# Chunk attention and a squared-ReLU FFN: V loads placed behind the transposes, one more square on ScalarE, one group a slot sooner

## The chip, the core and the metric

The kernel runs on one core of a Trainium2 chip. The metric is the device time of one execution in microseconds; the figure for the kernel before is the median of five executions.

## The reference

Attention is computed within chunks of 64 rows: every chunk of queries sees only the keys and values of its own chunk. The result is the input of a feed-forward layer whose activation is ReLU followed by a square.

```python
# q, k, v: (8, 8, 576, 64) float32;  chunk = 64, nine chunks per sequence
scores = scale * q_c @ k_c.T              # 64 x 64 per chunk and head
attn   = softmax(scores)
out    = attn @ v_c
x = out.transpose(0, 2, 1, 3).reshape(4608, 512)
h = maximum(x @ w_in, 0)                  # w_in  512 x 2048
y = (h * h) @ w_out                       # w_out 2048 x 512, y is float32
```

## The kernel before

**Tiles and blocks.** The 4608 tokens are cut into 18 groups of 256 tokens, and two groups make a block, so there are nine blocks, j = 0 to 8, of 512 tokens. A group is four chunks. Groups 14 and 15 (block 7) collect the ninth chunk of each sequence, so their loads come in smaller pieces than those of the other groups.

**Phases of a block.** `ffn_in(j)` computes 16 tiles of d_ff: four matmuls of 512 columns (L399), a ReLU on ScalarE (L410, PSUM to the tile `rl`), and the square (into `gT`), which is either a multiply on VectorE (L415) or an activation on ScalarE (L413). Which of the two is told by the tile's number. Blocks 2 to 8 take the tiles in the order `FT_EARLY` = 8, 0, 9, 1, 10 to 15, 2 to 7, and their list for ScalarE is `SQUARES_ON_ACT_EARLY` = (9, 10, 12). Then `ffn_out(j)` multiplies by w_out. In block 0 that is 64 plain matmuls (`ffn_out_by_ft`, L568). From block 1 on it is a scheme of the Strassen kind: seven products of half-size matrices (L468, 112 matmuls of 256 columns), on two PSUM accumulators called n and m. Their order is n, m, n (with d5), m (with d2), n (with d1), m (with d6), n (with d7). d1, d2, d5, d6 and d7 are differences of quarters of `gT`, made by VectorE (L384, tiles named `w_st`). The first two tiles of each are subtracted early, the other six just before `ffn_out` begins (`rest_of`).

**Attention beside the FFN.** The attention of later groups is spread over the blocks before them in steps: `C` casts q and k to bf16 (L259 and L262, on ScalarE from group 8 on), `TD` transposes them by DMA into `qkT` (L268), `SC` makes the scores (L291) and the exponential (L302), `AV` multiplies by V (L318) and normalises on VectorE (L325 and L326, result `x`), and `XT` transposes x into `xT`, the input of `ffn_in` (L339 by DMA from group 6 on, before that on TensorE at L345 with a copy at L350). The first groups are transposed on TensorE instead (`TA`, `TQ`, `TK`, L202 with copies at L211).

**What sets the order.** The schedule is written by hand. Each yield of a phase is a slot; ffn_in of a whole block has 16 slots and ffn_out has 14. After each slot at most one pending load is issued on SyncE's queue if the slot is in `go_slots`, and then the steps that `plan` holds for the slot are issued. Each engine, and each queue, does its instructions in program order, and waits only by semaphores. SyncE's queue holds no matmul, so a slot only sets where a load stands among the queue's other entries (the DMA transposes above all). In blocks 2 to 6 the loads of block j are q and k, and then V, of block j+2; V is read by `AV` in block j+1, and its buffers (`ve_sb`, `vo_sb`, lines 148 and 152) hold five groups. In blocks 2 to 7 the next block's steps stand at these slots (block 2 has slightly later ones):

```python
slots = {SC: (8, 8), AV: (11, 15), XT: (14, 18), C: (18, 20), TD: (20, 23)}
```

The outputs are stored from POOL's queue, and in blocks 2, 3 and 8 from SyncE's.

Of the kernel before, what the change touches and what calls it, by code (L numbers as in the profile page):

```python
# [17 lines left out]
def kernel(  # L18
# [22 lines left out]
    blocks = [[g, g + 1] for g in range(0, n_grp, 2)]  # L41
# [11 lines left out]
    FIRST_DMA_T = 4  # L53
    FIRST_DMA_X = 6
    SQUARES_ON_ACT = (10, 14, 3)
    SQUARES_ON_ACT_EARLY = (9, 10, 12)
    BT = GT * max(len(b) for b in blocks)

    const_pool = ctx.enter_context(tc.tile_pool(name="const", bufs=1))
# [96 lines left out]
    def go(pieces):  # L156
        for f in pieces:
            f()
# [194 lines left out]
    SC, AV, XT = scores, values, transpose_x  # L353
# [38 lines left out]
    def ffn_in(j, parts):  # L392
        if j not in gTs:
            gTs[j] = ffn_pool.tile([128, n_ft, BT], BF16, name="gT")
        gT, xT = gTs[j], xTs[j]
        for u, (c, n, fts, ft) in enumerate((*p, ft) for p in parts for ft in p[2]):
            h = ps_ffn.tile([128, 512], FP32, name="ps_ffn")
            for dt in range(n_dt):
                nc.tensor.matmul(  # L399
                    out=h[:, 0:n],  # L400
                    lhsT=w_in_bf[:, dt, ft * 128:(ft + 1) * 128],
                    rhs=xT[:, c // 128:(c + n) // 128, dt, :],
                    start=(dt == 0), stop=(dt == n_dt - 1))
            if j < 3:
                if n == 512 or u % 2 == 0:
                    rl_tile = ffn_pool.tile([128, 512], FP32, name="rl", bufs=3).bitcast(BF16)
                rl = rl_tile[:, u % 2 * 512:] if n < 512 else rl_tile
            else:
                rl = ffn_pool.tile([128, 512], FP32, name="rl", bufs=3)
            nc.scalar.activation(out=rl[:, 0:n], in_=h[:, 0:n], func=AF.Relu)  # L410
            on_act = SQUARES_ON_ACT_EARLY if fts is FT_EARLY else SQUARES_ON_ACT
            if (n == 512 and ft in on_act) or (n < 512 and (j == 0 or ft in (12, 3))):
                nc.scalar.activation(out=gT[:, ft, c:c + n], in_=rl[:, 0:n], func=AF.Square)  # L413
            else:
                nc.vector.tensor_tensor(  # L415
                    out=gT[:, ft, c:c + n], in0=rl[:, 0:n], in1=rl[:, 0:n], op=ALU.mult)
            if fts is FT_EARLY and u == 8:

                for name in ("d5", "d2", "d1", "d6", "d7"):
                    difference(j, name, slice(0, N_EARLY))  # L420
            yield
# [11 lines left out]
    def sum_quarters(out, in0, in1, op=ALU.add, half=slice(None)):  # L433
        return lambda _: add(nc.vector, out[:, half], in0[:, half], in1[:, half], op)
# [126 lines left out]
    def ffn_out_by_ft(j):  # L561

        gT = gTs.pop(j)
        n_tt = len(blocks[j]) * GT // 128
        o_ps = [ps_ffn.tile([128, d_model], FP32, name="ps_ffn") for _ in range(n_tt)]

        def mm(tt, ft):
            nc.tensor.matmul(  # L568
                out=o_ps[tt],
                lhsT=gT[:, ft, tt * 128:(tt + 1) * 128],  # L570
                rhs=w_out_bf[:, ft, :],
                start=(ft == 0), stop=(ft == n_ft - 1))


        for ft in range(n_ft - 4):
            for tt in range(n_tt - 1 if ft == 0 else n_tt):
                mm(tt, ft)
                if ft == 1 and tt == n_tt - 2:
                    mm(n_tt - 1, 0)
            yield  # L580
        for tt in range(n_tt):
            for ft in range(n_ft - 4, n_ft):
                mm(tt, ft)
            o_sb = ffn_pool.tile([128, d_model], FP32, name="o_sb", bufs=4)
            nc.scalar.copy(out=o_sb, in_=o_ps[tt])
            b, s0 = chunks[blocks[j][tt // 2]][0]
            t0 = b * S + s0 + tt % 2 * 128
            nc.gpsimd.dma_start(out=out[t0:t0 + 128, :], in_=o_sb)
            yield

    def pieces(grps):
        for g in grps:
            yield from qk_pieces(g)
        for g in grps:
            yield from v_pieces(g)
# [43 lines left out]
    for j, grps in enumerate(blocks):  # L639
        nxt = blocks[j + 1] if j + 1 < len(blocks) else []  # L640
        far = blocks[j + 2] if j + 2 < len(blocks) else []
        plan = {}

        def at(slot, f, g):
            plan.setdefault(slot, []).append((f, g))

        if j == 0:
            loads, go_slots = itertools.chain(*map(qk_pieces, far)), range(17)
            at(28, sum_quarters(b11_p_b21, b11, b21), None)
            for slot, f in ((24, TA), (27, SC), (29, AV), (31, XT)):  # L650
                at(slot, f, nxt[0])
            at(31, TQ, nxt[1])
            at(31, sum_quarters(b11_m_b22, b11, b22, ALU.subtract), None)
            phases = [first_ffn_in, ffn_out_by_ft(0)]
        elif j == 1:
            loads = itertools.chain(*map(v_pieces, nxt), *map(qk_pieces, far))
            go_slots = [*range(22, 27), *range(28, 48)]
            for slot, f in ((1, TK), (4, SC), (7, AV), (12, XT)):
                at(slot, f, grps[1])
            for i, g in enumerate(nxt):  # L660
                for slot, f in ((16 + 4 * i, C), (21 + 6 * i, TD), (36 + i, SC), (38 + 2 * i, AV),
                                (42 + i, XT)):
                    at(slot, f, g)
            for i, g in enumerate(far):
                at(36 + 4 * i, C, g)
                at(42 + 3 * i, TD, g)
            at(2, sum_quarters(b11_p_b12, b11, b12), None)
            at(12, sum_quarters(b12_p_b22, b12, b22), None)
            at(20, sum_quarters(b21_p_b22, b21, b22), None)
            phases = [ffn_in(1, [(0, 256, FT_ORDER), (256, 256, FT_ORDER)]), ffn_out(1)]  # L670
        else:
            loads, go_slots = pieces(far), range(32)
            slots = {SC: (8, 8), AV: (11, 15), XT: (14, 18), C: (18, 20), TD: (20, 23)}
            if j == 3:
                go_slots = [*range(6), *range(13, 32)]
            if j == 2:
                loads = itertools.chain(*map(v_pieces, nxt), loads)
                slots = {SC: (8, 10), AV: (12, 15), XT: (15, 18), C: (20, 23), TD: (22, 25)}
                go_slots = [*range(16), 23, 24, *range(26, 36)]
            for f in (SC, AV, XT):  # L680
                for i, g in enumerate(nxt):
                    at(slots[f][i], f, g)
            for f in (C, TD):
                for i, g in enumerate(far):
                    at(slots[f][i], f, g)
            phases = [ffn_in(j, [(0, BT, FT_EARLY)]), ffn_out(j)]
        slot = 0
        for phase in phases:
            for _ in phase:
                if slot in go_slots:  # L690
                    for f in loads:
                        f()
                        break
                for f, g in plan.get(slot, []):
                    f(g)
                slot += 1
        assert all(x < slot for x in plan), (j, slot, sorted(plan))
        go(loads)
# [30 lines left out]
```

The softmax here doesn't subtract the row's maximum and nothing guards it: scores larger than these inputs give would overflow.

## Time and profile before

| what | value |
|---|---|
| median of 5 executions | 282.61 us (281.75 to 283.49) |
| the profiled execution, its own time | 282.25 us |
| its span | 280.5 us |
| TensorE (PE) busy | 269.0 us, 96% |
| VectorE (DVE) busy | 189.4 us, 68% |
| ScalarE (ACT) busy | 161.9 us, 58% |
| GpSimd (POOL) busy | 48.5 us, 17% |
| granted TensorE clock | 9 or more tenths in every slice |

The profiled execution lies 0.36 us under the median. Its span leaves out 1.75 us around the first and last instruction. PE is the matmul row and PEld the row of weight loads, which run beside it; matmuls are pipelined, so a busy PE can still be waiting between two starts. A row of the timeline reads: start, duration, engine, line, operation, output<-input, count, and in brackets the idle time before it with what ended it. SPq is SyncE's queue.

In the trace block 3 runs from 110.97 to 139.00 us, block 4 to 167.04, block 5 to 195.08, block 6 to 223.11, block 7 to 251.15.

### The profile page before, as it was taken

How to read it: one execution, taken by the hardware profiler on the slowest of the kernel's cores; microseconds unless marked ns; L12 is line 12 of the kernel's file. 1: busy time of each engine (PE TensorE's matmuls, PEld its weight loads, DVE VectorE, ACT ScalarE, POOL GpSimd, SP SyncE). 2: the span in 40 equal slices, each digit the busy share in tenths (PEclk: the TensorE clock that was granted, in tenths of full speed). 3: DMA queues.
4: the chain of work that ended last, by engine and by line, in shares of the span. 5: the costliest groups of instructions: out<-in, count | busy, mean ns of one | idle time of the engine just before them, and what ended most of it. 6: DMA issues, size and time to landing. Idle time of an engine off the chain costs nothing.

```text
span 280.5 us, 7199 instructions
## 1 busy us (share of the span) xinstructions
PE 269.0 (96%) x2951; PEld 175.7 (63%) x2954; DVE 189.4 (68%) x338; ACT 161.9 (58%) x278; POOL 48.5 (17%) x79
## 2 busy tenths in 40 slices
PE   1999999999999999999999999999999999999995
PEld 1554454788784488448844884488448844884584
DVE  1255705898952795499549954995499549954983
ACT  1458705777349763977197719771977197219610
POOL 2038833350370000000000030003000300051000
PEclk9999999999999999999999999999999999999999
DMA  7999999999999999999999999169797970432003
GB/s 198 243 321 353 377 347 247 327 235 206 239 222 250 226 216 223 260 249 168 204 310 205 198 269 257 38 138 221 225 248 166 197 182 2 75 96 56 0 28 124
DMA packets 143072, 57.09 MB, mean 204 GB/s; under 512 B 110656, under 2 KB 140480, under 8 KB 143040
## 3 DMA queue, kind: packets, MB, share of 16 engines
q1 hardware_dynamic: 140768, 50.15, 78.5%
q0 software_dynamic: 1984, 6.29, 6.9%
q8 instruction: 23, 0.38, 0.6%
q10 hardware_dynamic: 288, 0.20, 0.2%
q14 instruction: 9, 0.07, 0.1%
HBM read 36.70 MB, written 9.44 MB: 165 GB/s over the span
## 4 chain that ended last, share of the span: by engine, by line
PE 65%; DVE 21%; ACT 6%; issue 3%; DMA 3%; SPq 1%; ACTq 0%
PE ps_ffn L468 29%; PE ps_ffn L399 25%; DVE gT L415 9%; ACT rl L410 5%; DVE x L326 5%; PE ps_ffn L568 5%; DVE w_st L384 4%; DMA k_sb<-in_k_dram 2%; PE ps_ffn L249 1%; PE ps_att L291 1%; PE ps_ffn L202 1%; PE ps_att L318 1%; DVE rec L325 1%; DMA vo_sb<-in_v_dram 1%; ACT gT L413 1%
## 5 line engine op out<-in xcount | busy, mean ns | idle before, releaser
L399 PE MATMUL ps_ffn<-xT,w_in_bf 128*128 128x512 bf16 (+1 forms) x648 | 129.4, 356 | 0.9 <-ACT rl L410 0.7
L415 DVE TENSOR_TENSOR gT<-rl 128x512 bf16<-128x512 f32 (+2 forms) x130 | 73.7, 604 | 53.7 <-ACT rl L410 53.5
L410 ACT ACTIVATE rl<-ps_ffn 128x512 f32<-128x512 f32 (+2 forms) x162 | 85.3, 549 | 22.9 <-PE ps_ffn L399 19.6
L399 PEld LDWEIGHTS <-w_in_bf 128*128 128x128 bf16 x648 | 61.7, 98 | 58.6 <-issue 0.8
L468 PEld LDWEIGHTS <-w_st 128*128 128x128 bf16 x640 | 61.7, 98 | 9.0 <-DVE w_st L384 1.8
L384 DVE TENSOR_TENSOR w_st<-gT 128x1536 bf16<-128x1536 bf16 (+2 forms) x75 | 50.3, 720 | 0.0
L468 PE MATMUL ps_ffn<-w_out_bf,w_st 128*128 128x256 bf16 x384 | 45.9, 273 | 0.4
L496 POOL DMA_DIRECT2D out_dram<-o_sb x16 | 11.4, 715 | 132.5 <-DVE o_sb L431 128.8
L468 PE MATMUL ps_ffn<-w_sum,w_st 128*128 128x256 bf16 x256 | 29.6, 273 | 0.0
L548 ACT COPY o_sb<-ps_ffn 128x512 f32<-128x512 f32 (+1 forms) x8 | 4.5, 558 | 40.9 <-PE ps_ffn L468 40.9
L468 PEld LDWEIGHTS <-gT 128*128 128x128 bf16 x256 | 24.5, 98 | 3.3
L326 DVE TENSOR_TENSOR x<-ps_att,rec 128x512 bf16<-128x512 f32 x36 | 24.9, 692 | 1.2
L302 ACT ACTIVATE e<-ps_att 128x1024 bf16<-128x1024 f32 x18 | 17.8, 1023 | 6.0 <-PE ps_att L291 6.0
L413 ACT ACTIVATE gT<-rl 128x512 bf16<-128x512 f32 (+2 forms) x32 | 18.4, 576 | 1.0
L468 PE MATMUL ps_ffn<-w_sum,gT 128*128 128x256 bf16 x128 | 15.3, 273 | 0.0
L468 PE MATMUL ps_ffn<-w_out_bf,gT 128*128 128x256 bf16 x128 | 15.3, 273 | 0.0
L568 PE MATMUL ps_ffn<-w_out_bf,gT 128*128 128x512 bf16 x61 | 14.2, 380 | 0.3 <-issue 0.2
L170 POOL CAST w_in_bf<-w_st 128x512 bf16<-128x512 f32 (+2 forms) x12 | 9.6, 819 | 18.1 <-DMA w_st<-in_moe_w_in_dram 17.9
L512 ACT COPY n<-ps_ffn 128x512 f32<-128x512 f32 (+1 forms) x9 | 4.8, 538 | 12.0 <-PE ps_ffn L468 12.0
L318 PEld LDWEIGHTS <-e 64*64 64x64 bf16 x576 | 6.5, 107 | 7.4 <-ACT rl L410 2.5
L259 ACT CAST qkb<-q_sb 128x1024 bf16<-128x1024 f32 x10 | 10.5, 1048 | 0.0
L262 ACT CAST qkb<-k_sb 128x1024 bf16<-128x1024 f32 x10 | 10.5, 1046 | 0.0
(53 smaller groups left out, 158.1 us busy)
## 6 DMA issues: line engine op xcount, KB each, us to landing
q_sb<-in_q_dram SPq DMA_DIRECT2D x16, 512.0 KB, 6.2
k_sb<-in_k_dram SPq DMA_DIRECT2D x24, 256.0 KB, 6.1
out_dram<-o_sb POOLq DMA_DIRECT2D x20, 256.0 KB, 4.6
ve_sb<-in_v_dram SPq DMA_DIRECT2D x32, 128.0 KB, 4.0
w_st<-in_moe_w_in_dram SPq DMA_DIRECT2D x8, 512.0 KB, 6.3
w_st<-in_moe_w_out_dram SPq DMA_DIRECT2D x8, 512.0 KB, 5.8
vo_sb<-in_v_dram SPq DMA_DIRECT2D x24, 128.0 KB, 3.5
out_dram<-o_sb SPq DMA_DIRECT2D x9, 256.0 KB, 3.2
```

What stands on the lines that cost most here:

```text
L259: copy(out=qkb[:, 0].rearrange("p (i h d) -> p i h d", i=2, h=H), in_=q_sb.rearrange("p (h i d) -> p i h d", h=H, i=2))
L262: copy(out=qkb[:, 1], in_=k_sb)
L302: nc.scalar.activation(out=e_out, in_=s_in, func=AF.Exp, scale=scale)
L326: nc.vector.tensor_tensor(out=x[:, t].rearrange("p h a d -> p a h d"), in0=o[:, :, :, 0:D], in1=rec.to_broadcast([128, 2, n_hp, D]), op=AL ...
L384: nc.vector.tensor_tensor(out=state[name, j][:, part], in0=x, in1=y, op=ALU.subtract)
L399: nc.tensor.matmul(out=h[:, 0:n], lhsT=w_in_bf[:, dt, ft * 128:(ft + 1) * 128], rhs=xT[:, c // 128:(c + n) // 128, dt, :], start=(dt == 0) ...
L410: nc.scalar.activation(out=rl[:, 0:n], in_=h[:, 0:n], func=AF.Relu)
L413: nc.scalar.activation(out=gT[:, ft, c:c + n], in_=rl[:, 0:n], func=AF.Square)
L415: nc.vector.tensor_tensor(out=gT[:, ft, c:c + n], in0=rl[:, 0:n], in1=rl[:, 0:n], op=ALU.mult)
L468: nc.tensor.matmul(out=outs[t], lhsT=a[:, i, t * 128:(t + 1) * 128], rhs=b[:, i, :], start=(first and i == 0 and (last or t == 0)), stop=( ...
L496: dma.dma_start(out=out[t0:t0 + HT, col:col + HD].rearrange("(t p) d -> p t d", p=128), in_=o_sb.rearrange("p (t d) -> p t d", d=HD))
L568: nc.tensor.matmul(out=o_ps[tt], lhsT=gT[:, ft, tt * 128:(tt + 1) * 128], rhs=w_out_bf[:, ft, :], start=(ft == 0), stop=(ft == n_ft - 1))
```

## The change

There are three edits. Tile 7, the last of d_ff in the order of blocks 2 to 8, is squared by ScalarE and no longer by VectorE. In block 0 the scores, values and x transpose of group 2 stand one slot sooner each. In blocks 4, 5 and 6 the loads of V go out from slot 24 on, which puts them behind all DMA transposes (`XT` at 14 and 18, `TD` at 20 and 23) in SyncE's queue; q and k keep slots 0 to 5 (0 to 15 in block 5, whose loads for block 7 come as 16 pieces), and what is left at the end of the block goes out there.

```diff
-    SQUARES_ON_ACT_EARLY = (9, 10, 12)
+    SQUARES_ON_ACT_EARLY = (9, 10, 12, 7)
...
         if j == 0:
...
-            for slot, f in ((24, TA), (27, SC), (29, AV), (31, XT)):
+            for slot, f in ((24, TA), (26, SC), (28, AV), (30, XT)):
                 at(slot, f, nxt[0])
             at(31, TQ, nxt[1])
...
             if j == 3:
                 go_slots = [*range(6), *range(13, 32)]
+            elif j > 3:
+
+                go_slots = [*range(16 if j == len(blocks) - 4 else 6), *range(24, 32)]
```

## The prediction

> **What bounds the kernel now.** I read the share of busy time first, then a table of stretches with one row for each block, then what TensorE's two rows waited for, and then the timeline around each wait.
>
> ```profile
> PE 269.0 (96%) x2951; PEld 175.7 (63%) x2954; DVE 189.4 (68%) x338; ACT 161.9 (58%) x278; POOL 48.5 (17%) x79
> ...
> 110.97:139.00 28.03, 27.96 (x305) 18.18 (x304) 20.81 (x36) 17.98 (x28) 0.00 (x0) 1.00 1.04 222
> 139.00:167.04 28.04, 27.96 (x306) 18.17 (x304) 20.81 (x36) 17.98 (x28) 2.14 (x3) 1.00 1.07 244
> 167.04:195.08 28.04, 27.96 (x305) 18.18 (x304) 20.81 (x36) 17.98 (x28) 2.85 (x4) 1.00 0.69 164
> ```
>
> PE is busy nearly all the time, and the block periods agree within 0.01 us, although the DMA share (second number from the end) goes from 1.07 to 0.69. So TensorE's own work sets the period, not the loads. 64 matmuls of 512 columns at a start-to-start pace of 0.2155 us are 13.8, 112 of 256 columns at 0.109 are 12.2, scores and values some 1.6: 27.6 of 28.03. There is no more to win in a block than a few tenths, and they must be waits of TensorE.
>
> ```profile
> PEld L468 <- DVE w_st L384: 1.8, 5, 0.4
> PEld L399 <- DVE xT L350: 0.4, 1, 0.4
> ```
>
> The first wait occurs five times. It is in blocks 3 to 7, at the same place in each (130.31, 158.35, 186.39, 214.42 and 242.46 us, by the chain that ended last). The timeline of block 4 shows it:
>
> ```profile
> 155.66 0.20 DVE L325 RECIPROCAL rec<-ps_att 128x8 f32<-128x8 f32 x1
> 155.90 0.69 DVE L326 TENSOR_TENSOR x<-ps_att,rec 128x512 bf16<-128x512 f32 x1
> 156.51 0.20 DVE L325 RECIPROCAL rec<-ps_att 128x8 f32<-128x8 f32 x1
> 156.74 0.69 DVE L326 TENSOR_TENSOR x<-ps_att,rec 128x512 bf16<-128x512 f32 x1
> 157.35 1.81 DVE L384 TENSOR_TENSOR w_st<-gT 128x1536 bf16<-128x1536 bf16 x2
> ...
> 157.78 0.21 PEld L468 LDWEIGHTS <-w_st 128*128 128x128 bf16 x2
> 158.35 0.33 PEld L468 LDWEIGHTS <-w_st 128*128 128x128 bf16 x4 [0.36 <-DVE w_st L384]
> ...
> 154.10 0.60 ACT L410 ACTIVATE rl<-ps_ffn 128x512 f32<-128x512 f32 x1 [0.27 <-PE ps_ffn L399]
> 156.35 0.58 ACT L512 COPY n<-ps_ffn 128x512 f32<-128x512 f32 x1 [1.65 <-PE ps_ffn L468]
> ```
>
> VectorE has a backlog: the last squares, then AV's normalisation, then d5. TensorE has used d5's two early tiles and waits for the other six; two matmul starts lie 0.351 us apart where 0.109 is the pace. ScalarE idles 1.65 us in the same stretch. The second wait is at the border of blocks 0 and 1:
>
> ```profile
> 49.02 0.61 PE L345 MATMUL ps_att<-ident,x 128*128 128x128 bf16 x8
> 49.56 0.64 PE L202 MATMUL ps_att<-ident,q_sb 128*64 128x128 bf16 x16
> 49.67 0.69 DVE L350 COPY xT<-ps_att 128x1024 bf16<-128x1024 bf16 x1 [0.63 <-PE ps_att L345]
> 50.42 0.83 PE L399 MATMUL ps_ffn<-xT,w_in_bf 128*128 128x256 bf16 x6 [0.21 <-DVE xT L350]
> ```
>
> The last transpose starts at 49.98, the first matmul of block 1 at 50.42: 0.435 us, where such a step takes 0.06.
>
> **The change, part by part.**
>
> *Tile 7 on ScalarE, seven times.* It removes a multiply of 0.688 us from VectorE (group row of L415, f32; 0.60 from start to start) and adds a Square of 0.630 (row of L413). Tile 7 is the last of ffn_in, so the ReLU of it ends at 154.70, the Square would end at 155.33, and the next entry on ScalarE, the copy of n at 156.35, waits for TensorE anyway: 1.0 us of cover remains. Without that cover the copy, the casts behind it and the second copy of n would be late by up to 0.63. On VectorE rec, x and d5 move up 0.60: d5 ends at 157.69 in place of 158.29, and TensorE asks for it at 158.00. So the wait goes whole: five starts of 0.345, 0.351, 0.349, 0.349 and 0.352, less 0.109 each, are **1.20 us**. Blocks 2 and 8 show no such start, so nothing there. What is late next is ScalarE's second copy of n (L521): four casts stand before it, it ends at 161.20, and TensorE's product with d1, which overwrites the running sum of n, starts at 161.64, or 161.39 when 0.24 is gone. A handover takes 0.055 (d5's end to the weight load), which leaves 0.14 of slack. In block 7 no casts stand there.
>
> The skill speaks against one more Square: ScalarE: Activation LUTs, What ACT_TABLE_LOAD costs, says that each switch to a different set of functions costs about 2.66 us. At two switches for each of seven Squares the sum would be +37 us, an estimate by that page. The group of such loads in the trace counts one, of 1283 ns, at the start, while 32 Squares stand among ReLUs, copies and exponentials. I take the row: no switch.
>
> *Group 2 a slot sooner.* The same instructions: 32 score matmuls and an exponential, 32 value matmuls with two rec and two x, eight transposes and the copy of xT. None is a DMA (group 2 is transposed on TensorE), so SyncE's and POOL's queues are as before. Each step passes four matmuls of L568 on TensorE (0.86 us). SC then starts at 43.82 in place of 44.68; its operands are copied by 43.17. AV starts at 46.03; its exponential ends near 45.4, the b11+b21 sum ahead of it on VectorE ends at 45.33, and its last V lands at 45.43, so 0.6 is left. XT comes at 48.15, x keeps its distance, and xT is copied near 49.5, under the last four L568 and the 16 transposes of q. The first matmul of block 1 moves from 50.42 to about 50.05: **0.37 us**. From there the chain runs through VectorE to 62.8 (squares, weight sums, no slack). Its head is the ReLU at 53.04, which follows the copy of k (52.08), which follows TensorE. VectorE itself moves up only 0.13, since its q copy starts at 50.15 in place of 50.28, but it idled 0.38 before the square at 53.47, so 0.13 of slack remains and the whole 0.37 passes on.
>
> *V behind the transposes, blocks 4 to 6.* No instruction more or less; 9, 16 and 9 loads go behind two xT and two qkT transposes, and the q and k of the next block behind them. In block 4 the transposes no longer queue behind V (the first was ready at 153.4 and issued at 156.13). Counting issue times as they stand in SyncE's rows, the last qkT goes out near 160.8, V by 168, q and k for block 7 by 178 (before: 174.8, and the last at 182.8 both ways). V of block 6 is read at 178; block 7's V would land by 204 and its first group is read at 206.1, with that group's own pieces in by 200; block 8's V would land by 228 and be read at 234.2. The casts that read q and k stand at 184.9 and 212.9, with some 4 us to spare. On the other side, a qkT that today lands at 230.06, for scores at 230.8, lands near 222. Nothing on TensorE waits for any of these today, so I take **0**. V now meets POOL's stores; cover gone, each us of late V costs one. DMA: Bandwidth & Descriptors, Queues, rings and completion order, says that the engines take turns between queues packet by packet. By it 1 MB of V beside 1 MB of stores takes double: at the 244 GB/s of block 4's row 8.2 us in place of 4.1 (estimate). In the trace the transpose at 220.59, beside stores, took 6.6 us to issue and 9.5 to land, against a median of 4.6, so also double. Either leaves V in time; the sum is 0 by both. Bounds: −0.2 to +3.8.
>
> **Sum.** 1.20 + 0.37 = 1.57 us: 282.25 becomes 280.68 for the profiled execution. That one lies 0.36 under the median, so I predict 282.61 − 1.57 = **281.0**, 0.56% less.
>
> **The rivals.** (1) *Block 0's gain is swallowed* by the VectorE-bound first half of block 1, or V of group 2 lands 0.6 later. For: 0.13 us of slack in VectorE. Against: the idle 0.38. Time: 281.4. (2) *The wait moves to ScalarE's copy of n* before d1. For: 0.14 of slack. Against: that is still slack. With half of block 3 to 6's gain lost: 282.61 − 1.57 + 0.5 = 281.5. (3) *Slower: V comes late.* If in block 6 the last qkT issue takes 6.6 us again, at 216.8, and the nine V behind it 1.5 each beside the stores, the last lands near 240.5, where block 7's second AV wants it at 236.7: +3.8, so 284.8. It decides when V lands after 236.7. Against: the transposes then run before the stores start at 218.9, and V issues at 0.5 to 0.7 mostly. (4) *More:* the wait of TensorE for the exponential at 54.97 (0.2), and waits that other executions may have, go too: 280.4. That the slots don't delay V is no rival that matters: SyncE runs ahead of TensorE, so only the order counts, and its worth is 0.
>
> **How the numbers follow.** Forecast 0.60; swallowed 0.13; copy of n 0.12; late V 0.08; more 0.07. The forecast's own spread is 280.7 to 281.4. About 0.5% (1.41 us, 281.2) is what a measurement of this kernel can tell from no change. Faster: 0.48 of the forecast and the 0.07 of (4), 0.55. Same: 0.12 of the forecast, and (1) and (2), 0.37. Slower: 0.08. The range from 280.3 to 282.3 leaves out late V and some tails.
>
> **What would show it.** The wait of L468's weight loads for w_st falls from 1.8 to about 0, blocks 3 to 7 take 27.8 us, L413 counts 39 and L415 123; block 1 starts near 50.05 with no wait for xT; V stands behind L268 in SyncE's rows. Wrong, if a wait for n, L521, or for ve_sb or vo_sb appears on TensorE.

## The result and the profile after

The changed kernel takes 281.2 us (median of 30 executions, 279.97 to 282.39), the kernel before 282.3 (51 executions, 281.24 to 286.2). The ratio is 0.9947, with a 95% interval from 0.9933 to 0.9962, so 0.53% less; the medians alone lie 1.1 us, 0.39%, apart. This ratio leaves out executions over 1.5% above the fastest of their kernel; the counts of long executions further down leave out none. The profiled execution took 280.45 us against 282.25, its span 278.53 against 280.46: 1.9 us, more than the median moved.

The first part of the page, the share of busy time:

```profile
PE 267.8 (96%) x2951; PEld 175.8 (63%) x2954; DVE 184.6 (66%) x331; ACT 165.9 (60%) x285; POOL 47.0 (17%) x79
```

Seven instructions went from VectorE (338 to 331) to ScalarE (278 to 285). The table of stretches, cut at the first matmul of blocks 3 to 8 (columns: stretch, length, busy PE, PEld, DVE, ACT, POOL, granted clock, DMA share, GB/s):

```profile
110.11:137.90 27.79, 27.79 (x306) 18.25 (x304) 20.21 (x35) 18.61 (x29) 0.00 (x0) 1.00 1.03 228
137.90:165.69 27.79, 27.79 (x307) 18.27 (x305) 20.21 (x35) 18.61 (x29) 1.99 (x3) 1.00 1.03 225
165.69:193.47 27.78, 27.78 (x307) 18.24 (x304) 20.20 (x35) 18.61 (x29) 2.85 (x5) 1.00 0.93 203
193.47:221.25 27.78, 27.78 (x306) 18.23 (x304) 20.20 (x35) 18.61 (x29) 2.85 (x5) 1.00 0.98 213
221.25:249.04 27.79, 27.79 (x306) 18.25 (x304) 20.20 (x35) 14.93 (x25) 3.73 (x7) 1.00 0.38 91
```

Every block is 0.24 to 0.26 us shorter: 1.25 in all. The timeline of block 4 at the place of the old wait:

```profile
153.79 0.63 ACT L413 ACTIVATE gT<-rl 128x512 bf16<-128x512 f32 x1
154.13 0.20 DVE L325 RECIPROCAL rec<-ps_att 128x8 f32<-128x8 f32 x1
155.41 0.58 ACT L512 COPY n<-ps_ffn 128x512 f32<-128x512 f32 x1 [0.99 <-PE ps_ffn L468]
155.81 1.82 DVE L384 TENSOR_TENSOR w_st<-gT 128x1536 bf16<-128x1536 bf16 x2
156.84 1.74 PEld L468 LDWEIGHTS <-w_st 128*128 128x128 bf16 x16
```

The Square runs in what was ScalarE's idle time (1.65 us before the copy of n, 0.99 now). d5 is the first of the two subtractions in VectorE's last row. It is done at 156.76, before the first of these weight loads, and the loads run through without a bracket.

The border of blocks 0 and 1 in TensorE's and VectorE's timeline:

```profile
48.34 0.61 PE L345 MATMUL ps_att<-ident,x 128*128 128x128 bf16 x8
48.79 1.03 PE L568 MATMUL ps_ffn<-w_out_bf,gT 128*128 128x512 bf16 x4
48.99 0.69 DVE L350 COPY xT<-ps_att 128x1024 bf16<-128x1024 bf16 x1 [0.75 <-PE ps_att L345]
49.74 0.64 PE L202 MATMUL ps_att<-ident,q_sb 128*64 128x128 bf16 x16
50.32 1.05 PE L399 MATMUL ps_ffn<-xT,w_in_bf 128*128 128x256 bf16 x8
```

The copy of xT is covered and the wait for it is gone, but block 1 starts only 0.10 us earlier than before (50.42). And SyncE's queue in block 6, first before, then after:

```profile
214.88 1.16 SPq L152 DMA_DIRECT2D vo_sb<-in_v_dram  x2
216.14 2.67 SPq L339 DMA_TRANSPOSE xT<-x  x2
218.90 8.31 SPq L268 DMA_TRANSPOSE qkT<-qkb  x2
...
208.64 4.96 SPq L339 DMA_TRANSPOSE xT<-x  x2
213.70 4.04 SPq L268 DMA_TRANSPOSE qkT<-qkb  x2
217.79 1.19 SPq L148 DMA_DIRECT2D ve_sb<-in_v_dram  x2
```

The transposes now come first, and the two of qkT take 4.04 us to issue in place of 8.31.

Where the 1.9 us of this profile come from: 1.25 in blocks 3 to 7, 0.16 in block 0 (first L568 to first L399 of block 1: 17.16 us, before 17.32), and 0.59 in block 1's ffn_in (50.32 to 66.94, before 50.42 to 67.63), less 0.06 by which the first matmul starts later. The 0.59 was no step of the prediction. The experiments take these apart.

### The profile page after: what moved, and what is told of

Same layout as the page of the kernel before. It is cut to its first block, busy times and chain, and to the rows that moved or that the text cites. A ratio compares the mean times of both kernels' runs of the same rounds, so it can differ in the third digit from the quotient of the medians.

```text
span 278.5 us, 7178 instructions
## 1 busy us (share of the span) xinstructions
PE 267.8 (96%) x2951; PEld 175.8 (63%) x2954; DVE 184.6 (66%) x331; ACT 165.9 (60%) x285; POOL 47.0 (17%) x79
## 4 chain that ended last, share of the span: by engine, by line
PE 89%; SPq 4%; DMA 2%; DVE 1%; ACT 1%; issue 1%; POOL 0%; ACTq 0%
PE ps_ffn L399 43%; PE ps_ffn L468 36%; PE ps_ffn L568 5%; PE ps_att L318 2%; DMA w_st<-in_moe_w_in_dram 2%; PE ps_att L291 2%; SPq L148 1%; SPq L106 1%; SPq L152 1%; DVE gT L415 1%; ACT rl L410 1%; PE ps_att L202 1%; PE ps_att L345 0%; DVE w_out_bf L431 0%; ACT e L302 0%
## 5 line engine op out<-in xcount | busy, mean ns | idle before, releaser
L399 PE MATMUL ps_ffn<-xT,w_in_bf 128*128 128x512 bf16 (+1 forms) x648 | 129.5, 356 | 0.5 <-POOL w_in_bf L170 0.4
L415 DVE TENSOR_TENSOR gT<-rl 128x512 bf16<-128x512 f32 (+2 forms) x123 | 69.4, 599 | 53.5 <-ACT rl L410 53.2
L399 PEld LDWEIGHTS <-w_in_bf 128*128 128x128 bf16 x648 | 61.6, 98 | 58.2 <-POOL w_in_bf L170 0.6
L468 PE MATMUL ps_ffn<-w_out_bf,w_st 128*128 128x256 bf16 x384 | 45.1, 273 | 0.0
L468 PEld LDWEIGHTS <-gT 128*128 128x128 bf16 x256 | 24.5, 98 | 3.3
L413 ACT ACTIVATE gT<-rl 128x512 bf16<-128x512 f32 (+2 forms) x39 | 22.9, 586 | 1.2
L568 PE MATMUL ps_ffn<-w_out_bf,gT 128*128 128x512 bf16 x61 | 14.2, 380 | 0.4 <-issue 0.3
L259 ACT CAST qkb<-q_sb 128x1024 bf16<-128x1024 f32 x10 | 10.5, 1048 | 0.0
L262 ACT CAST qkb<-k_sb 128x1024 bf16<-128x1024 f32 x10 | 10.5, 1046 | 0.0
L568 PEld LDWEIGHTS <-gT 128*128 128x128 bf16 x64 | 6.0, 98 | 6.8
```

The costliest lines, as they stand in the source:

```text
L259: copy(out=qkb[:, 0].rearrange("p (i h d) -> p i h d", i=2, h=H), in_=q_sb.rearrange("p (h i d) -> p i h d", h=H, i=2))
L399: nc.tensor.matmul(out=h[:, 0:n], lhsT=w_in_bf[:, dt, ft * 128:(ft + 1) * 128], rhs=xT[:, c // 128:(c + n) // 128, dt, :], start=(dt == 0) ...
L415: nc.vector.tensor_tensor(out=gT[:, ft, c:c + n], in0=rl[:, 0:n], in1=rl[:, 0:n], op=ALU.mult)
L468: nc.tensor.matmul(out=outs[t], lhsT=a[:, i, t * 128:(t + 1) * 128], rhs=b[:, i, :], start=(first and i == 0 and (last or t == 0)), stop=( ...
L568: nc.tensor.matmul(out=o_ps[tt], lhsT=gT[:, ft, tt * 128:(tt + 1) * 128], rhs=w_out_bf[:, ft, :], start=(ft == 0), stop=(ft == n_ft - 1))
```

## The experiments

Theory: the square brings 1.2 us, block 0 little, V what executions lose to late transposes; the 0.59 us of block 1 is chance. The rivals are in the expectations.

### The square alone

```diff
-    SQUARES_ON_ACT_EARLY = (9, 10, 12)
+    SQUARES_ON_ACT_EARLY = (9, 10, 12, 7)
```

> Only tile 7's square moves to ScalarE. Theory (the square is worth the five waits for d5): blocks 3 to 7 take 27.79 us each, 1.2 us less in all, ratio 0.9957; no wait of L468's weight loads for w_st. Rival (the five waits were only part of it, and the gain needs V behind the transposes too): blocks of about 27.9 and under 0.8 us less, ratio 0.997 or more.

281.9 us, ratio 0.9964 (0.9940 to 0.9988). The wait for w_st is gone from all five blocks. But the stretches of its blocks 5 and 6 are longer than 27.79:

```profile
138.57:166.35 27.78, 27.78 (x307) 18.27 (x304) 20.21 (x35) 18.62 (x29) 1.99 (x3) 1.00 1.03 225
166.35:194.29 27.94, 27.94 (x306) 18.35 (x304) 20.21 (x35) 18.68 (x29) 2.84 (x5) 1.00 1.12 202
194.29:222.28 27.99, 27.96 (x307) 18.18 (x304) 20.21 (x35) 18.61 (x30) 3.01 (x5) 1.00 0.95 219
222.28:250.08 27.80, 27.80 (x305) 18.26 (x306) 20.20 (x35) 14.93 (x25) 3.59 (x6) 1.00 0.42 92
```

For the 27.99 of block 6 its timeline gives the reason, at the first weight load of block 7:

```profile
222.27 0.76 PEld L399 LDWEIGHTS <-w_in_bf 128*128 128x128 bf16 x5 [0.31 <-DMA xT<-x]
```

TensorE comes to the block's border before the DMA transpose of x, which here stands behind V, has landed. The 27.94 of block 5 is a late transpose too:

```profile
174.21 0.87 PE L291 MATMUL ps_att<-qkT 64*64 64x64 bf16 x64
```

The second half of these scores starts at 174.63, 0.17 us after the matmul before it; the qkT that it reads was issued at 166.78, behind V, and landed at 174.59. So both theories are partly right: the square is worth 1.25 where nothing else is late, and here 0.37 of it went to transposes behind V (blocks 3 to 7 take 139.30 us, against 138.93 in the changed kernel). Whether they were late because TensorE is faster, or by the scatter of executions, this one profile does not tell; the table further down speaks for the scatter.

### Block 0 alone

```diff
-            for slot, f in ((24, TA), (27, SC), (29, AV), (31, XT)):
+            for slot, f in ((24, TA), (26, SC), (28, AV), (30, XT)):
```

> Only group 2's scores, values and x transpose stand a slot sooner. Theory (of the predicted 0.37 us some 0.15 is left, and the 0.6 us that block 1 lost in the changed kernel's profile is the chance of when POOL's casts meet VectorE): 0.1 to 0.3 us less, ratio 0.9990 to 0.9997, block 1's long start gap of TensorE still there in some executions. Rival (the slot causes block 1's gain): 0.75 us less, ratio 0.9973.

282.6 us, ratio 1.0019 (0.9992 to 1.0046): no gain that can be measured. In its profile block 0 is 0.27 us shorter (17.05), but ffn_in of block 1 takes 17.26 us, against 17.21 before, so the slot does not cause the changed kernel's 16.62.

### V alone

```diff
             if j == 3:
                 go_slots = [*range(6), *range(13, 32)]
+            elif j > 3:
+                go_slots = [*range(16 if j == len(blocks) - 4 else 6), *range(24, 32)]
```

> Only V stands behind the transposes in blocks 4 to 6. Theory: TensorE's starts as before, the profile's span as before within 0.7 us, ratio of the medians 0.999 to 1.0; but if some executions wait for the qkT that lands 0.8 us ahead of its scores in block 7, the executions over 283.4 us (14 of 51 before) become fewer. Rival (V is worth nothing in any execution): as many over 283.4 as before, ratio 1.0.

281.98 us, ratio 0.9995 (0.9975 to 1.0016). The five waits for d5 are all there (starts of 0.347 to 0.358), the span is 280.4. Three of 22 executions lie over 283.4, of before 14 of 75 beside it: alone no proof. (The 14 of 51 in the expectation is 12.)

### Square and block 0, without V

> The changed kernel without the V part: square and block 0. Theory: its profile's span is that of the changed kernel within 0.7 us (278.5), ratio 0.995 to 0.996; executions far above its median appear again if V is what takes them away. Rival (V behind the transposes carries part of the 0.53%): ratio 0.997 or more.

281.95 us, ratio 0.9979 (0.9954 to 1.0004), its span 279.4, not 278.5. Of the 0.9 us between the spans 0.64 is block 1's ffn_in (17.26 against 16.62), which V does not touch. But TensorE's waits name xT twice:

```profile
PEld L399 <- DMA xT<-x: 0.5, 2, 0.3
```

One is at the start of block 5 (166.59), behind block 4's V, and costs 0.21 us. The other is at the start of block 3, where the change leaves the queue as it was. Six of 22 executions lie over 283.4, of the changed kernel none of 30. The ratio is on the rival's side (0.997 or more), though its interval still overlaps the changed kernel's: V behind the transposes probably carries a part.

### Square and V, without block 0

> The changed kernel with group 2's steps at their old slots: the square and the V part alone. Theory (block 0's edit is worth 0.1 to 0.3 us, the square 1.24, V a few tenths in the median by taking late transposes away): blocks 3 to 7 all 27.79 us, no wait for xT, ratio 0.9945 to 0.9965, and at most one execution in twenty over 283.4. Rival (V is worth nothing): ratio and scatter as of the square alone, 0.9964, with a fifth over 283.4.

280.83 us, ratio 0.9952 (0.9930 to 0.9974), no execution over 283.4 (the longest is 282.01). That is the changed kernel's time without block 0's edit. Its blocks were not all 27.79: 27.79, 27.97, 27.79, 27.98 and 27.78. The expectation of 27.79 in all five and of no wait for xT missed: at the start of block 3 TensorE waited for an xT that landed at 110.95, and went on at 111.00. In block 6 the prediction's "late next" shows:

```profile
215.71 1.05 ACT L262 CAST qkb<-k_sb 128x1024 bf16<-128x1024 f32 x1 [0.23 <-DMA k_sb<-in_k_dram]
216.66 0.58 ACT L521 COPY n<-ps_ffn 128x512 f32<-128x512 f32 x1
217.29 0.92 PE L468 MATMUL ps_ffn<-w_sum,w_st 128*128 128x256 bf16 x7
```

A load of k lands late, the cast waits 0.23 us, the copy of n behind it ends at 217.24, and the product with d1 starts then, 0.2 us late: rival (2), in one block of one execution. It is a cost of the V edit, since q and k now queue behind the V of the block before. The last k of block 6 landed 3.5, 2.1 and 3.9 us ahead of its cast before, with the square alone and with block 0 alone; with V behind the transposes it landed 0.3 to 0.6 us ahead in four profiles (0.3 in the changed kernel), and late here. Block 2, which the change hardly touches, waited 0.6 us for a qkT in this profile. Block 4's extra 0.18 us lies inside the second group's values matmuls (a start of 0.164 near 154.3), though their V had landed by 143.03; its cause stays open.

The pairs with and without V: before 282.37 to 281.98, square 281.9 to 280.83, square and block 0 281.95 to 281.2. V is worth 0.4, 1.1 and 0.75 us in the median. By the ratios it is 0.1, 0.3 and 0.9 us, and in each pair the intervals overlap, so V's worth for a middling execution is not clear of noise. The long executions are clearer. Of the executions without the V part (before, beside the result and the three sets of experiments, and three of the kernels), 68 of 280 lie over 283.4; with it (the changed kernel, V alone, square and V, and the sums moved, below) 3 of 82. The threshold favours kernels that are faster anyway by 1.2 us; over 3 us above their own fastest lie 39 and 2. (With the second kernel of the next pair and the two with changed casts, which all have V behind, it is 4 of 144.)

The profiles show the same. This table gives how long before its use a transpose landed, in us (xT: the last one, before the block's first matmul; qkT: the second one, before its scores; 0.04 or 0.05 means that TensorE waited for it; a dash, that the landing is missing in the trace):

| profile | xT, block 5 | qkT, block 5 | xT, block 7 | qkT, block 7 |
|---|---|---|---|---|
| before | 5.62 | 9.75 | 2.14 | 1.03 |
| block 0 alone | 2.07 | 0.77 | 2.60 | 3.42 |
| square alone | 1.54 | 0.04 | 0.05 | 1.36 |
| square and block 0 | 0.05 | 0.66 | 1.97 | 1.00 |
| V alone | – | 10.31 | 5.83 | 9.99 |
| square and V | 6.77 | 10.10 | 5.09 | 8.38 |
| changed kernel | 6.74 | 10.04 | – | 9.72 |

With V ahead, each profile has a transpose with 1.03 us of slack or less, and at the old pace of TensorE the slack of one and the same transpose differs by 3.6 us (5.62 and 2.07) and by 9 us (9.75 and 0.77) between two profiles. With V behind, none has less than 5.09. In blocks 2 and 3, where V still goes ahead of the transposes or between them, the changed kernel keeps the old risk: block 3's xT had 2.88 us in the changed kernel and 0.05 in square and V.

### How much a late transpose costs, and a late V

Two pieces of V of group 16 are loaded twice in block 6. The second load writes the same buffer, so it waits for the first to land and holds the queue some 3 us. Once with V ahead of the transposes (the kernel without the V part), once behind (the changed kernel).

```diff
     def v_pieces(g):
-        for t, p, m, b, s in runs(g):
+        for t, p, m, b, s in [r for r in runs(g) for _ in range(2 if g == 16 else 1)]:
```

> The changed kernel without the V part, and only the two even pieces of V of group 16 issued twice in block 6. Each second load waits for the first to land, some 3 us, so V ahead of the transposes holds them up by 5 to 6 us. Theory: xT of block 7 lands near 225 us, TensorE waits 2.5 to 4.5 us for it at the border of blocks 6 and 7, and the time is 285 or more. Rival (a delay of the transposes is hidden anyway): no such wait, under 282.5.

> The changed kernel, with the same two pieces issued twice, behind the transposes. Theory: V of group 16 lands near 230 and of group 17 near 234 us, wanted near 232 and 236, so TensorE waits under 0.5 us and the time is that of the changed kernel, 281.2, within 0.7 us. Rival (the same delay costs as much on V as on the transposes): a wait for V in block 7 and 283.5 or more.

Ahead: 289.1 us (four executions), ratio 1.0239 (1.0179 to 1.0298), and a wait for xT of 7.4 us, where 2.5 to 4.5 were expected. Behind: 281.17 us, 0.9962 (0.9939 to 0.9985), no wait for V in block 7, the changed kernel's time. Two executions of 20 were over 283.4. The queue and TensorE of the first:

```profile
210.13 8.46 SPq L148 DMA_DIRECT2D ve_sb<-in_v_dram  x4
221.79 1.70 SPq L339 DMA_TRANSPOSE xT<-x  x1
225.57 1.28 SPq L339 DMA_TRANSPOSE xT<-x  x1
...
229.30 0.13 PEld L399 LDWEIGHTS <-w_in_bf 128*128 128x128 bf16 x2 [7.68 <-DMA xT<-x]
229.31 2.31 PE L399 MATMUL ps_ffn<-xT,w_in_bf 128*128 128x512 bf16 x5 [7.41 <-DMA xT<-x]
```

And the queue of the second:

```profile
210.72 4.24 SPq L339 DMA_TRANSPOSE xT<-x  x2
215.42 3.62 SPq L268 DMA_TRANSPOSE qkT<-qkb  x2
219.09 6.75 SPq L148 DMA_DIRECT2D ve_sb<-in_v_dram  x4
```

The same two loads cost over 7 us ahead of the transposes and nothing behind them. This shows what a delay there costs; that the long executions of before are such delays is likely, but no long execution was profiled.

A first version of this pair loaded all nine pieces of groups 16 and 17 twice, which, behind the transposes, put the last V 22 us later, in place of the 5 us of delay that I expected.

```diff
+        ... for _ in range(2 if g >= 16 else 1)   # both in runs(g) and in odd_loads[g]
```

> The changed kernel without the V part, and V of groups 16 and 17 (block 6's loads) issued twice. Theory (V ahead of the transposes holds up xT and qkT of block 7, and TensorE feels it once their 1 to 2 us of slack are gone): nine more issues of about 0.6 us put both xT some 5 us later, so TensorE waits 2 to 5 us for xT at the start of block 7, or for qkT at its scores; 2 to 5 us slower than the changed kernel. Rival (V has nothing to do with what TensorE waits for): no wait for xT or qkT there, within 0.5 us of the changed kernel without the V part.

> The changed kernel, and V of groups 16 and 17 issued twice, behind the transposes. Theory: the transposes stand ahead of it, V of group 17 lands near 233 us against the values step that reads it near 236, so no wait of TensorE and the time of the changed kernel within 0.5 us. Rival (late V is what costs): TensorE waits for ve_sb or vo_sb in block 7, 1 us or more slower.

296.9 and 297.3 us. Ahead TensorE waits 14.4 us for xT, behind 10.5 us for V in five pieces. Both expectations missed, since the second load waits for the first. But the second shows where rival (3) of the prediction begins: counted from the start of block 7, the last V lands after 6.5 us in the changed kernel, after 10.3 with two pieces doubled, which is free, and after 28.9 here, which costs what late transposes do.

### Block 1: POOL's casts and VectorE

Block 1's ffn_in takes 17.21 us before, 17.23, 17.26, 17.10 and 17.26 in the first four experiments, and 16.62 in the changed kernel's profile. It is none of the three edits: the kernel with two pieces doubled ahead of the transposes has the same instructions as square and block 0 up to block 6, and its block 1 takes 16.73 us in place of 17.26; square and V takes 16.70, with an unchanged block 0. The difference is where POOL's casts fall. Of the kernel before, POOL's, VectorE's and TensorE's rows:

```profile
59.44 1.19 POOL L259 CAST qkb<-q_sb 128x1024 bf16<-128x1024 f32 x1 [0.46 <-DMA q_sb<-in_q_dram]
61.21 1.39 POOL L262 CAST qkb<-k_sb 128x1024 bf16<-128x1024 f32 x1 [0.59 <-DMA k_sb<-in_k_dram]
...
59.65 2.05 DVE L431 TENSOR_TENSOR w_out_bf<-w_out_bf 128x2048 bf16<-128x2048 bf16 x1
61.62 1.32 DVE L415 TENSOR_TENSOR gT<-rl 128x256 bf16<-128x256 bf16 x2
...
63.27 0.49 PE L399 MATMUL ps_ffn<-xT,w_in_bf 128*128 128x256 bf16 x3 [0.65 <-ACT rl L410]
```

And of the changed kernel:

```profile
56.40 1.04 POOL L259 CAST qkb<-q_sb 128x1024 bf16<-128x1024 f32 x1 [5.13 <-DMA q_sb<-in_q_dram]
...
56.55 0.69 DVE L326 TENSOR_TENSOR x<-ps_att,rec 128x512 bf16<-128x512 f32 x1
59.78 1.21 DVE L431 TENSOR_TENSOR w_out_bf<-w_out_bf 128x2048 bf16<-128x2048 bf16 x1
...
61.79 1.91 PE L399 MATMUL ps_ffn<-xT,w_in_bf 128*128 128x256 bf16 x14
```

A sum or square that reads two tiles from SBUF and begins under a cast is not done until the cast is: a square ends 0.14 us after it and takes up to 1.12 us in place of 0.28, the sum takes 2.05 in place of 1.21. The normalisation, which reads PSUM, is not held up (0.69 both ways). The first cast starts when a load of q lands (54.25 before, 56.40 here), so it differs between profiles of the same instructions; whether by execution or by chip is open, since the first four experiments ran on one chip and the later ones on others. Four such operations are long before TensorE's pause near 62 us in the kernel before, two in the changed kernel, and the chain that ended last runs through them and a ReLU to the matmul at 63.27. It fits a lock that the Trainium skill names (SBUF — State Buffer, SBUF: two separate sides: between GpSimd and a VectorE operation with two inputs in SBUF, whichever starts first has the ports for the whole instruction). The experiment casts k of groups 4 and 5 three times:

```diff
         copy(out=qkb[:, 1], in_=k_sb)
+        if g in (4, 5):
+            copy(out=qkb[:, 1], in_=k_sb)
+            copy(out=qkb[:, 1], in_=k_sb)
```

> The changed kernel, and the cast of k of groups 4 and 5 on POOL done three times in place of once: four more POOL casts in block 1. Theory (a POOL cast makes one VectorE square or sum that it overlaps 0.8 us longer, and block 1's first half is VectorE's): three or four more squares of about 1.1 us, block 1 longer by 1 to 3 us. Rival (the long squares come from elsewhere, and POOL costs nothing): as many long squares as before, time within 0.5 us.

284.28 us, ratio 1.0062 (1.0043 to 1.0081), 3.1 us over the changed kernel. Seven squares are long in place of three, and block 1's ffn_in takes 19.98 us. VectorE's row (lines are three higher in this kernel):

```profile
60.51 5.69 DVE L418 TENSOR_TENSOR gT<-rl 128x256 bf16<-128x256 bf16 x7
```

Seven squares in 5.69 us, where free ones start 0.20 apart and seven take 1.5. Two tries to get out of it followed. First, the casts of groups 4 and 5 on ScalarE:

```diff
-        copy = nc.gpsimd.tensor_copy if g < 8 else nc.scalar.copy
+        copy = nc.gpsimd.tensor_copy if 6 <= g < 8 else nc.scalar.copy
```

> The changed kernel with the casts of groups 4 and 5 on ScalarE in place of POOL. Theory: no square in the first half of block 1 takes over 0.5 us, and TensorE's long start near 62 us is gone for good; but ScalarE gets 4.2 us of casts in a block where it is busy 14.4 of 17.8 us, so block 1 is between 0.6 us shorter and 1.5 us longer than now. Rival (POOL's casts don't matter): long squares stay.

283.2 us, ratio 1.0034 (1.0018 to 1.0051). Block 1's ffn_in takes 19.16 us, 2.5 more than in the changed kernel, where at most 1.5 more was expected. No square is long, as the theory has it, but now TensorE waits for ScalarE's ReLU, which stands behind the casts:

```profile
62.91 1.91 PE L399 MATMUL ps_ffn<-xT,w_in_bf 128*128 128x256 bf16 x16 [0.94 <-ACT rl L410]
66.34 0.92 PE L399 MATMUL ps_ffn<-xT,w_in_bf 128*128 128x256 bf16 x7 [1.52 <-ACT rl L410]
```

Second, less work for VectorE in the crowded half:

```diff
-            at(12, sum_quarters(b12_p_b22, b12, b22), None)
-            at(20, sum_quarters(b21_p_b22, b21, b22), None)
+            at(20, sum_quarters(b12_p_b22, b12, b22), None)
+            at(27, sum_quarters(b21_p_b22, b21, b22), None)
```

> The changed kernel with the sum b12+b22 at slot 20 and b21+b22 at slot 27 of block 1, in place of 12 and 20. Theory (VectorE is late by 0.7 us or so in block 1's first half and idles 0.9 us near 66 to 67 us, so 1.2 us of sum moved past that point costs nothing): no start of TensorE over 0.5 us in block 1 in any cast timing, block 1 from 0 to 0.7 us shorter, ratio to before 0.992 to 0.995. Rival (the sum is late for product m, or the squares' backlog only moves): a wait of L468 for w_out_bf or as long as now, ratio 0.995 or more.

280.99 us, ratio 0.9947 (0.9921 to 0.9974). In its profile TensorE has no long start near 62 us (one of 0.45 near 58), and block 1's ffn_in takes 16.72 us although four squares are lengthened; but square and V takes 16.70 there without this edit. It isn't distinguishable from the changed kernel, so it is no proven gain; nothing tried beats the changed kernel clearly.

## Why the prediction was right

The time, 281.0 for 281.2, and 0.56% for 0.53%, were right, and the largest term, the square, was right in its mechanism. The other two terms were wrong in opposite directions, and that they offset each other is luck. So is part of the nearness in time: the five executions that the 282.61 came from lay high, and from the 282.3 of 51 executions the same 1.57 us gives 280.7.

- *The square, 1.20 us: right.* It measured 1.25, with d5 done before TensorE asks, ScalarE's idle time 0.99 in place of 1.65 (1.0 of cover was forecast), and no loading of tables.
- *Block 0, 0.37 us: too large.* 0.16 was left in the profile (0.27 and 0.10 in two others), and nothing that can be measured in the time. In the seven later profiles with this edit block 0 took from 17.03 to 17.93 us, against 17.31 or 17.32 in the four without it. The step "AV starts at 46.03; ... its last V lands at 45.43, so 0.6 is left" failed: in the profile after, V landed at 46.34, and the second half of AV started 0.13 late. In seven of the ten profiles with the edit it waits like that, by up to 0.39, and in none of the four without it. The rest is that TensorE goes from x's transposes to L568 and then to q's transposes, where before the two stood together; "the whole 0.37 passes on" failed too, since what comes out of block 1 depends on the casts. Rival (1) is what happened to it.
- *V, 0: too small.* The step "Nothing on TensorE waits for any of these today, so I take 0" failed twice. It read one execution, in which the second qkT was 1.0 us ahead of the scores that read it (the 0.8 is against the first scores of the block); a quarter of the executions of before were over 283.4 us, and with V behind the transposes 3 of 82. And in both profiles of the square with V ahead, transposes were late, at a cost of 0.37 and 0.2 us; whether the faster pace or the scatter did that is not shown. The pairs give V 0.4 to 1.1 us in the median, not clear of noise. Rival (4) had the place ("waits that other executions may have").
- *Late V, rival (3): not seen.* The slack was as counted: block 6's last V landed at 227.76, for the forecast 228, and even 3.8 us more are free. Double loads show the price far beyond it.
- *Copy of n, rival (2): seen once*, at 0.2 us. The step "with some 4 us to spare" for q and k was wrong: in block 6 of the changed kernel the last k landed at 214.00, and its cast began at 214.29.

## What to carry to other kernels

A step that costs no TensorE time in one profile can still be worth its slack: look at how much time lies between a transfer's landing and its use, and compare that with the spread of the executions. When transfers are reordered, count the slack of every transfer again, of those that moved back too: here the second qkT of block 7 went from 1.0 us of slack to 9.7, and the last k of block 6 from 3.5 to 0.3. And where two engines share a block, list which of their operations overlap, before a difference between two profiles is taken for an effect of the change.

## What the runs showed of the hardware

After the wait of 7.4 us in the kernel with V twice ahead, TensorE ran at half its pace. The table of stretches over the wait, the 4.2 us after it, and the rest:

```profile
221.65:229.30 7.65, 0.25 (x3) 0.00 (x0) 0.00 (x0) 0.58 (x1) 0.96 (x2) 0.83 1.19 269
229.30:233.50 4.20, 4.19 (x10) 1.46 (x11) 0.69 (x1) 1.16 (x2) 0.00 (x0) 0.51 0.90 204
233.50:250.00 16.50, 16.50 (x212) 9.12 (x211) 12.57 (x25) 12.60 (x22) 0.00 (x0) 1.00 0.09 18
```

Most of the ten matmuls start 0.427 us apart in place of 0.2155, at a granted clock of 0.51. The wait of 7.4 us so cost 2.0 us more: block 7 takes 29.83 us in place of 27.79. The same pace followed, for some 5 us each, a wait of 14.0 us in the first version with V ahead, and two waits of 1.75 and 3.04 us close together in the one with V behind. Waits of up to 1.5 us, as in the kernel with casts on ScalarE, did not do that. It is why a transpose that is several microseconds late is dearer than its lateness.
